# Transposing two raw row tiles on TensorE, with the mean subtracted in PSUM, and first load groups of four feature tiles

## The chip, the cores and the metric

The kernel runs on one core of one Trainium2 chip. The core has five engines with a queue of their own each: TensorE (PE, matmuls; its weight loads are shown as PEld), VectorE (DVE), ScalarE (ACT), GpSimd (POOL) and SyncE (SP), which here only issues DMAs. The engines run side by side and wait for each other through semaphores; each works through its own instructions in the order in which the program gives them. The metric is the device time of one execution in microseconds; lower is better.

## The reference

The input x has 2048 rows of 512 features, in bf16. Its rows are layer-normalized, and two branches run on the normalized rows:

```python
xn = _layernorm(x, axis=-1)
return x + _A_ref(xn, ...) + _B_ref(xn, B_w_gate, B_w_up, B_w_down)

# A: a diagonal state space model, 512 complex states, scanned over the 2048 rows
h = Lam_bar[None, :] * h + Bu[:, t, :]
y = 2.0 * jnp.einsum("blp,dp->bld", hseq, Cmat).real + x * Dskip[None, None, :]
# B: a gated network with 1376 inner features
g = _silu(x @ w_gate)
u = x @ w_up
return (g * u) @ w_down
```

## The kernel before, in words

The 2048 rows are 16 row tiles of 128, and four chunks of four tiles. The 1376 inner features are ten feature tiles of 128 and a rest of 96. For each chunk TensorE does a B projection (`bproj_chunk`, 32 matmuls, L382), the gate and up products (`gateup_chunk`, L457, and L508 for the rest of the features), and the output (`out_chunk`, L569 and L579). VectorE does the statistics, the scans of the state space model with rotations before and after them, and the products of gate and up. ScalarE evacuates PSUM, applies SiLU and computes sines.

Chunk 0 goes another way, so that TensorE can begin early. Its gate and up products take the transposed rows as the stationary operand (`sw_mm`, L484), in three groups of feature tiles (`fgroups`): 0 to 2, 3 to 6 and 7 to 9, so 384, 512 and 384 columns a matmul, 32 matmuls for each group. The weights of the first two groups are loaded in halves. The rows are only centred before they are transposed; the factor 1/std is applied by ScalarE when it evacuates the products (`sw_out`, L493 for the gate with SiLU, L494 for up), and the product of gate and up is taken for two row tiles at a time (L498). These products go to a staging tile `g0` and are transposed by DMA (`g0_dma`, L501).

The head, the code up to the first group's end, is written out by hand. Row tile 0 is summed by VectorE (L227) and centred in two halves as 512 x - sum (L234), which a factor `rs0` takes back later (L701); row tile 1 gets its mean from ScalarE (L230) and is centred by VectorE (L238), as are tiles 2 and 3 with means from the normal statistics (L193, L194). TensorE transposes a centred tile in four blocks (`cT_pe`, L250) and ScalarE copies the result to SBUF (`cT_copy`, L254). Dummy matmuls (L636) keep TensorE busy from the start. The bank allocations rotate through eight PSUM banks; `held` keeps the banks of the first group until `sw_out` reads them. The small vector of parameters is transposed by TensorE (L276) and cast by VectorE (L277); GpSimd takes powers, for 1/std (L203) and for the time steps `dt_t` (L280); VectorE then makes `dre` (L283) and the arguments of the two small sines (`params_sin`, L335 and L337 on ScalarE). The fully normalized rows of chunk 0 (L211) are transposed by DMA (`xT_dma`, L260) for its B projection.

After the head a planner sets the order of VectorE's work. `queue` appends operations with an estimated cost to `backlog`; `pump(us)` is called after each stretch of TensorE work, adds that stretch's length to an account `owed`, and issues operations as long as `owed` is at least half the cost of the next one; `multiply` issues the waiting gate-up products and takes 0.65 from `owed` for each; `need(tag)` issues all that is left up to a tag. Behind the head the list holds: the sine tables of two quarters (L296, L302 to L305), the statistics of row tiles 4 to 7 (`ln1`), their normalization and transpose, and the rest of the tables. Each step of group 1 and group 2 pumps its own TensorE time; each step of a B projection pumps `BP`.

All early loads but three run in SyncE's queue in program order: tile 0, half a gate group, tile 2, half an up group, tile 3, then the second and third groups, row tiles 4 to 7 and the DMA transposes. ScalarE issues tile 1 and two of the halves.

Of the kernel before, what the change touches and what calls it, by code (L numbers as in the profile page):

```python
# [23 lines left out]
def kernel(  # L24
# [17 lines left out]
    nc = tc.nc  # L42
    _, L, D = A_x.shape
# [20 lines left out]
    const = ctx.enter_context(tc.tile_pool(name="const", bufs=1))  # L64
# [9 lines left out]
    def bank(shape=(128, CW), dtype=F32):  # L74
        return psum.tile(list(shape), dtype, name="ps")
# [6 lines left out]
    wg_v = B_w_gate.rearrange("(k p) f -> p k f", p=128)  # L82
    wu_v = B_w_up.rearrange("(k p) f -> p k f", p=128)


    xall = const.tile([128, NT, D], BF16, name="xall")
    xnT = const.tile([128, NCH, KD, CW], BF16, name="xnT")

    fgroups = [(0, 3), (3, 7), (7, FT - 1)]
    wg_g, wu_g = [], []  # L90
    for gi, (a, b) in enumerate(fgroups):
        cols = min(F, b * 128) - a * 128
# [18 lines left out]
    def load_w1(q, tiles, view, gi):  # L111
        a, b = fgroups[gi]
        q.dma_start(out=tiles[gi][:], in_=view[:, :, a * 128:min(F, b * 128)])


    def load_w1_half(q, tiles, view, gi, k0, k1):
        a, b = fgroups[gi]
        q.dma_start(out=tiles[gi][:, k0:k1, :], in_=view[:, k0:k1, a * 128:min(F, b * 128)])

    HK = KD // 2  # L120
    nc.sync.dma_start(out=xall[:, 0, :], in_=x_v[:, 0, :])
    nc.vector.memset(xall[:, 1, 0:2], 0.0)
    nc.scalar.dma_start(out=xall[:, 1, :], in_=x_v[:, 1, :])
    load_w1_half(nc.sync, wg_g, wg_v, 0, 0, HK)
    nc.scalar.preload_act_table_set("silu_and_others")
    load_w1_half(nc.scalar, wg_g, wg_v, 0, HK, KD)
    nc.sync.dma_start(out=xall[:, 2, :], in_=x_v[:, 2, :])
    load_w1_half(nc.scalar, wu_g, wu_v, 0, 0, HK)
    load_w1_half(nc.sync, wu_g, wu_v, 0, HK, KD)
    nc.sync.dma_start(out=xall[:, 3, :], in_=x_v[:, 3, :])  # L130
    for tiles, view in ((wg_g, wg_v), (wu_g, wu_v)):
        load_w1_half(nc.sync, tiles, view, 1, 0, HK)
        load_w1_half(nc.sync, tiles, view, 1, HK, KD)
    load_w1(nc.sync, wg_g, wg_v, 2)
    load_w1(nc.sync, wu_g, wu_v, 2)
    prm_rows = const.tile([128, 128], BF16, name="prm_rows")
# [35 lines left out]
    ident = const.tile([128, 128], BF16, name="ident")  # L172
    make_identity(nc, ident[:])
    jidx = const.tile([128, CW], F32, name="jidx")


# [15 lines left out]
    def ln_stats(n):  # L192
        nc.vector.bn_stats(out=stats[:, n, 0, :], in_=xall[:, n, :])  # L193
        nc.vector.bn_aggr(out=mv[:, n, :], in_=stats[:, n, 0, :])  # L194
# [6 lines left out]
    def ln_rstd(a, b):  # L201
        nc.vector.tensor_scalar(out=ve[:, a:b], in0=mv[:, a:b, 1], scalar1=EPS, scalar2=None, op0=ALU.add)  # L202
        nc.gpsimd.tensor_tensor(out=rstd[:, a:b], in0=ve[:, a:b], in1=neg_half[:, 0:b - a], op=ALU.pow)  # L203
# [20 lines left out]
    rs0 = const.tile([128, 1], F32, name="rs0")  # L224

    def sum_dve(i):
        nc.vector.tensor_reduce(out=sums[:, 0:1], in_=xall[:, i, :], axis=mybir.AxisListType.X, op=ALU.add)  # L227

    def mean_act(i):
        nc.scalar.activation(out=xnT[:, NCH - 1, 0, :], in_=xall[:, i, :], func=ACT.Copy, scale=1.0 / D,  # L230
                             accum_out=sums[:, 1:2])

    def center_by_sum(i, lo, hi):
        nc.vector.tensor_scalar(out=xc[:, i, lo:hi], in0=xall[:, i, lo:hi], scalar1=float(D),  # L234
                                scalar2=sums[:, 0:1], op0=ALU.mult, op1=ALU.subtract)
# [4 lines left out]
    tA = bank((128, 2, KD, 128), BF16)  # L240
    tB = bank((128, 2, KD, 128), BF16)
    warm = bank()

    def cT_tile(i, k):
        return (((tA, 0) if k < HK else (tB, 0)), (tA, 1), (tB, 1), (tA, 0))[i]

    def cT_pe(i, k0=0, k1=KD):
        t, h = cT_tile(i, k0)
        for k in range(k0, k1):
            nc.tensor.transpose(out=t[:, h, k, :], in_=xc[:, i, k * 128:(k + 1) * 128], identity=ident[:])  # L250

    def cT_copy(i, k0=0, k1=KD):
        t, h = cT_tile(i, k0)
        nc.scalar.copy(out=xcT[:, k0:k1, i * 128:(i + 1) * 128], in_=t[:, h, k0:k1, :])  # L254

    def runs(ap):
        return ap.rearrange("p k (i t) -> p (k i) t", t=128)
# [14 lines left out]
    V = nc.vector  # L272

    def prm_transpose():
        pp = tA[:, 1, 0, :]
        nc.tensor.transpose(out=pp, in_=prm_rows[:], identity=ident[:])  # L276
# [210 lines left out]
    def sw_out(gi, i, psg, psu):  # L487
        a, b = fgroups[gi]
        w = (b - a) * 128
        scale = rs0[:] if i == 0 else rstd[:, i:i + 1]  # L490
        if i % 2 == 0:
            u_pair[0, gi] = up_p.tile([128, 2, CW], BF16, name="u2")
        nc.scalar.activation(out=g0[:, a:b, i, :], in_=by_k(psg[:, 0:w]), func=ACT.Silu, scale=scale)  # L493
        nc.scalar.activation(out=u_pair[0, gi][:, i % 2, 0:w], in_=psu[:, 0:w], func=ACT.Copy, scale=scale)  # L494
        if i % 2 == 1:
            g = g0[:, a:b, i - 1:i + 1, :]
            u = u_pair[0, gi][:, :, 0:w].rearrange("p i (f d) -> p f i d", d=128)
            products.append(lambda: V.tensor_tensor(out=g, in0=g, in1=u, op=ALU.mult))  # L498
# [132 lines left out]
    BP = 4 * 0.2163  # L631
    one = nc.const_aps.tensor(1.0, (128, 1), BF16)

    def dummy(n, cols):
        for _ in range(n):
            nc.tensor.matmul(warm[:, 0:cols], lhsT=one.to_broadcast([128, 128]), rhs=one.to_broadcast([128, cols]),  # L636
                             start=True, stop=True)

    def ln_rest(c, on_act):
# [15 lines left out]


    G, U = wg_g, wu_g
    held = [[None, None] for _ in range(TPC)]

    def head_mm(which, i, k0=0, k1=KD):  # L660
        if k0 == 0:
            held[i][which] = bank()
        sw_mm(held[i][which], (G, U)[which], 0, i, k0, k1)

    dummy(7, CW)
    dummy(3, 128)
    sum_dve(0)
    mean_act(1)
    center_by_sum(0, 0, HW)
    center_by_sum(0, HW, D)  # L670
    cT_pe(0, 0, HK)
    cT_copy(0, 0, HK)
    cT_pe(0, HK, KD)
    cT_copy(0, HK, KD)
    center(1, sums[:, 1:2])
    dummy(2, 128)
    cT_pe(1)
    cT_copy(1)
    head_mm(0, 0)
    ln_stats(1)  # L680
    ln_rstd(1, 2)
    ln_stats(2)
    center(2, mv[:, 2, 0:1])
    ln_rstd(2, 3)
    head_mm(0, 1)
# [15 lines left out]
    V.tensor_scalar(out=rs0[:], in0=rstd[:, 0:1], scalar1=1.0 / D, scalar2=None, op0=ALU.mult)  # L701
# [157 lines left out]
```

## Time and profile before

| what | value |
|---|---|
| median of 3 runs (lowest to highest) | 179.48 us (179.46 to 179.9) |
| the profiled execution's own time | 179.06 us |
| its span | 177.1 us |
| TensorE busy | 172.7 us (97%) |
| VectorE busy | 157.4 us (89%) |
| ScalarE busy | 108.5 us (61%) |
| GpSimd busy | 27.8 us (16%) |
| mean DMA rate over the span | 98 GB/s |
| first gate matmul of chunk 0 starts | 5.14 us |
| B projection of chunk 0, of chunk 1 starts | 23.31 us, 31.12 us |

Times within the trace count from the first instruction of the span. The span is shorter than the time of the execution, which also holds what lies around the program. A row of the timeline gives the start, the length, the engine, the line of the code, the operation, what it writes and reads, and how many instructions of the kind follow each other; in square brackets stands the idle time before it with what ended that. A line with a q behind the engine (SPq) is the issue of a DMA, not the transfer.

### The profile page before, as it was taken

To read this page: it belongs to the slowest core of one execution; us is meant where nothing else is said; L and a number is where in the kernel's file an instruction comes from. 1 tells how busy PE (TensorE), PEld (TensorE's weight loads), DVE (VectorE), ACT (ScalarE), POOL (GpSimd) and SP (SyncE) were. 2 spreads that over 40 slices of the span, in tenths; PEclk is the share of its full clock that TensorE was granted. 3 is DMA by queue.
4 is the path that set the end of the run, shared out by engine and by line. 5 is a ranking of instruction groups with operands and counts; after the bars stand their busy time and mean duration, and the time that the engine had idled before them with its cause. 6 is when DMAs were issued, how large, how long until landed. Compare 5 with 4: busy or idle time off the path is not lost.

```text
span 177.1 us, 2357 instructions
## 1 busy us (share of the span) xinstructions
PE 172.7 (97%) x851; PEld 81.9 (46%) x867; DVE 157.4 (89%) x258; ACT 108.5 (61%) x186; POOL 27.8 (16%) x36
## 2 busy tenths in 40 slices
PE   8999999999999999999999999999999999999993
PEld 3554544444444444444444444443444444444743
DVE  3978999999999999999999999999999996899033
ACT  4469998799976697036996660024866659771000
POOL 6370030050000000047000000025000002506100
PEclk9999999999999999999999999999999999999999
DMA  5999998999994000027033000007200002993612
GB/s 167 355 329 215 147 241 164 210 251 231 161 302 178 0 0 4 0 31 84 6 61 62 0 0 0 0 3 88 31 0 2 0 0 16 180 161 37 83 46 76
DMA packets 35115, 17.36 MB, mean 98 GB/s; under 512 B 24960, under 2 KB 35040, under 8 KB 35072
## 3 DMA queue, kind: packets, MB, share of 16 engines
q1 hardware_dynamic: 30672, 13.31, 33.9%
q0 software_dynamic: 3456, 3.28, 14.6%
q10 hardware_dynamic: 976, 0.62, 1.2%
q8 instruction: 7, 0.11, 0.3%
q14 instruction: 4, 0.03, 0.1%
HBM read 8.03 MB, written 5.24 MB: 75 GB/s over the span
## 4 chain that ended last, share of the span: by engine, by line
PE 97%; issue 1%; ACT 0%; DVE 0%
PE ps L457 29%; PE ps L569 22%; PE ps L382 16%; PE ps L579 16%; PE ps L484 10%; PE ps L636 2%; PE ps L508 2%; PE ps L518 1%; PE ps L250 1%; ACT CF L254 0%; DVE xall L582 0%; PE ps L276 0%
## 5 line engine op out<-in xcount | busy, mean ns | idle before, releaser
L569 PE MATMUL ps<-wd_sb,guT 128*128 128x512 bf16 (+4 forms) x195 | 38.6, 355 | 0.2
L457 PE MATMUL ps<-xnT,wg 128*128 128x512 bf16 x120 | 30.8, 380 | 0.1
L457 PE MATMUL ps<-xnT,wu 128*128 128x512 bf16 x114 | 30.0, 379 | 0.2
L424 DVE TENSOR_TENSOR_SCAN g<-r_t,car,u 128x512 bf16<-128x512 f32 x24 | 28.9, 1267 | 0.0
L382 PE MATMUL ps<-xnT,BT 128*128 128x512 bf16 x126 | 28.2, 380 | 0.2
L579 PE MATMUL ps<-CF,wt 128*128 128x512 bf16 (+2 forms) x140 | 28.1, 355 | 0.2
L569 PEld LDWEIGHTS <-guT 128*128 128x128 bf16 (+1 forms) x198 | 18.5, 98 | 19.9
L586 POOL DMA_DIRECT2D out_dram<-res x12 | 10.5, 1043 | 82.6 <-ACT res L585 76.3
L585 ACT CAST res<-ps 128x512 bf16<-128x512 f32 x12 | 7.0, 585 | 25.6 <-PE ps L579 23.3
L471 ACT ACTIVATE guT<-ps 128x512 bf16<-128x512 f32 x30 | 18.0, 601 | 5.1 <-PE ps L457 4.9
L472 ACT CAST u<-ps 128x512 bf16<-128x512 f32 x30 | 17.7, 590 | 5.2 <-PE ps L457 4.8
L384 ACT CAST u<-ps 128x512 bf16<-128x512 f32 x32 | 17.9, 595 | 4.6 <-PE ps L382 4.5
L579 PEld LDWEIGHTS <-wt 128*128 128x128 bf16 x144 | 13.5, 98 | 14.3
L382 PEld LDWEIGHTS <-BT 128*128 128x128 bf16 x128 | 12.5, 98 | 15.1 <-DMA xnT<-xn 0.4
L457 PEld LDWEIGHTS <-wg 128*128 128x128 bf16 x120 | 11.6, 98 | 14.5 <-issue 0.8
L457 PEld LDWEIGHTS <-wu 128*128 128x128 bf16 x120 | 11.7, 98 | 14.2
L541 ACT ACTIVATE xr<-xall,nb,rstd 128x512 bf16<-128x512 bf16 x16 | 11.9, 806 | 4.0 <-DVE xall L549 2.0
L484 PEld LDWEIGHTS <-CF 128*128 128x128 bf16 x96 | 9.1, 98 | 7.7 <-ACT CF L254 0.4
L203 POOL TENSOR_TENSOR rstd<-ve,neg_half 128x1 f32<-128x1 f32 (+1 forms) x7 | 7.8, 1118 | 26.0 <-DVE ve L202 26.0
L484 PE MATMUL ps<-wg,CF 128*128 128x384 bf16 (+1 forms) x47 | 10.7, 344 | 0.1
L484 PE MATMUL ps<-wu,CF 128*128 128x384 bf16 (+1 forms) x48 | 10.6, 344 | 0.0
L582 DVE TENSOR_TENSOR xall<-ps,xall 128x512 bf16<-128x512 f32 (+2 forms) x6 | 3.1, 514 | 8.1 <-remote 5.6
(110 smaller groups left out, 206.7 us busy)
## 6 DMA issues: line engine op xcount, KB each, us to landing
out_dram<-in_A_x_dram SPq DMA_DIRECT2D x1, 1536.0 KB, 7.7
out_dram<-res POOLq DMA_DIRECT2D x12, 128.0 KB, 3.2
out_dram<-xall POOLq DMA_DIRECT2D x3, 512.0 KB, 6.9
wd_sb<-in_B_w_down_dram SPq DMA_DIRECT2D x1, 1280.0 KB, 7.4
xall<-in_A_x_dram SPq DMA_DIRECT2D x1, 1024.0 KB, 6.6
wg<-in_B_w_gate_dram SPq DMA_DIRECT2D x2, 256.0 KB, 4.8
wu<-in_B_w_up_dram SPq DMA_DIRECT2D x2, 256.0 KB, 4.7
xall<-in_A_x_dram SPq DMA_DIRECT2D x1, 512.0 KB, 6.5
```

The lines of the kernel that those rows point to most:

```text
L203: nc.gpsimd.tensor_tensor(out=rstd[:, a:b], in0=ve[:, a:b], in1=neg_half[:, 0:b - a], op=ALU.pow)
L382: nc.tensor.matmul(ps[:], lhsT=BT[:, part, k, q * 128:(q + 1) * 128], rhs=xnT[:, c, k, :], start=(k == 0), stop=(k == KD - 1))
L384: nc.scalar.copy(out=u_tiles[c][:, part, q, :], in_=ps[:])
L424: V.tensor_tensor_scan(out=g()[:, part, q, :], data0=r_t[:, q:q + 1].to_broadcast([128, CW]), data1=u_tiles[c][:, part, q, :], initial=ini ...
L457: nc.tensor.matmul(ps[:fs, lo:hi], lhsT=wslice(groups, fi, k), rhs=xnT[:, c, k, lo:hi], start=(k == 0), stop=(k == KD - 1))
L471: nc.scalar.activation(out=guT[:fs, fi, :], in_=psg[:fs], func=ACT.Silu)
L472: nc.scalar.copy(out=u_pair[c][:fs, fi % 2, :], in_=psu[:fs])
L484: nc.tensor.matmul(ps[:, 0:(b - a) * 128], lhsT=xcT[:, k, i * 128:(i + 1) * 128], rhs=groups[gi][:, k, :], start=(k == 0), stop=(k == KD - 1))
L541: nc.scalar.activation(out=box["xr"][:], in_=xall[:, n, :], func=ACT.Identity, scale=rstd[:, n:n + 1], bias=nb[:, n:n + 1])
L569: nc.tensor.matmul(o[:], lhsT=gu_tiles[c][:fsz[fi], fi, i * 128:(i + 1) * 128], rhs=wd_sb[:fsz[fi], fi, lo:hi], start=(fi == 0), stop=False)
L579: nc.tensor.matmul(o[:], lhsT=w_tiles[c][:, part, q, i * 128:(i + 1) * 128], rhs=CF[:, part, q, lo:hi], start=False, stop=(part == 1 and q ...
L586: nc.gpsimd.dma_start(out=out_v[:, n, lo:hi], in_=res[:, lo:hi], accum_op=ALU.add)
```

## The change

Row tiles 0 and 1 are no longer centred before they are transposed. TensorE multiplies the raw tile by the identity (`cT_mm`, an ordinary matmul into an f32 bank, in place of a transpose into a bf16 one). Then one more matmul (`cT_mean`) subtracts the mean in the same bank: its stationary operand is a constant matrix of -1/512, its moving operand a diagonal matrix that holds the sum of each row, repeated over the blocks. VectorE sums tile 0 and makes its diagonal, ScalarE does both for tile 1. The copies out of PSUM are shared by VectorE and ScalarE. Tile 0 is now scaled like the others, so `rs0` and its instruction go. Tile 2 takes its mean from ScalarE, and its statistics come later. Tiles 2 and 3 are centred by VectorE as before and transposed by ordinary matmuls.

The feature groups become 0 to 3, 4 to 7 and 8 to 9, so 512, 512 and 256 columns a matmul. Both gate halves and both up halves of the first group are loaded by SyncE; ScalarE loads row tile 1 alone. The identity is made first on GpSimd. There are four long dummy matmuls in place of seven. The `sw_out` of tiles 0 to 3 for the first group stand at other places, and with them their products.

```diff
-    fgroups = [(0, 3), (3, 7), (7, FT - 1)]
+    fgroups = [(0, 4), (4, 8), (8, FT - 1)]
...
+    ident = const.tile([128, 128], BF16, name="ident")
+    make_identity(nc, ident[:])
+    minus_mean = const.tile([128, 128], BF16, name="minus_mean")
     nc.sync.dma_start(out=xall[:, 0, :], in_=x_v[:, 0, :])
     nc.vector.memset(xall[:, 1, 0:2], 0.0)
+    nc.vector.memset(minus_mean[:], -1.0 / D)
     nc.scalar.dma_start(out=xall[:, 1, :], in_=x_v[:, 1, :])
+    nc.scalar.preload_act_table_set("silu_and_others")
     load_w1_half(nc.sync, wg_g, wg_v, 0, 0, HK)
-    nc.scalar.preload_act_table_set("silu_and_others")
-    load_w1_half(nc.scalar, wg_g, wg_v, 0, HK, KD)
+    load_w1_half(nc.sync, wg_g, wg_v, 0, HK, KD)
     nc.sync.dma_start(out=xall[:, 2, :], in_=x_v[:, 2, :])
-    load_w1_half(nc.scalar, wu_g, wu_v, 0, 0, HK)
+    load_w1_half(nc.sync, wu_g, wu_v, 0, 0, HK)
     load_w1_half(nc.sync, wu_g, wu_v, 0, HK, KD)
...
+    def sum_act(i):
+        nc.scalar.activation(out=xnT[:, NCH - 1, 0, :], in_=xall[:, i, :], func=ACT.Copy, accum_out=sums[:, i:i + 1])
...
+    def diag_dve(i):
+        nc.vector.tensor_scalar(out=diag[:, i, :], in0=ident[:], scalar1=sums[:, i:i + 1], scalar2=None, op0=ALU.mult)
+
+    def diag_act(i):
+        nc.scalar.activation(out=diag[:, i, :], in_=ident[:], func=ACT.Copy, scale=sums[:, i:i + 1])
...
+    p2, p0, p1 = bank((128, KD, 128)), bank((128, KD, 128)), bank((128, KD, 128))
+    held = [[None, None] for _ in range(TPC)]
+    held[0][0], held[1][0], held[0][1], held[1][1], held[2][0] = (bank() for _ in range(5))
+
+    def cT_mm(ps, src, k, first, stop):
+        nc.tensor.matmul(ps[:, k, :], lhsT=src[:, k * 128:(k + 1) * 128], rhs=ident[:], start=first, stop=stop)
+
+    def cT_mean(ps, i, k0, k1):
+        nc.tensor.matmul(ps[:, k0:k1, :], lhsT=minus_mean[:],
+                         rhs=diag[:, i:i + 1, :].to_broadcast([128, k1 - k0, 128]), start=False, stop=True)
+
+    def cT_copy(copy, ps, i, k0=0, k1=KD):
+        copy(out=xcT[:, k0:k1, i * 128:(i + 1) * 128], in_=ps[:, k0:k1, :])
...
-    dummy(7, CW)
-    dummy(3, 128)
+    warm = held[2][0]
+    dummy(warm, 4, CW)
+    dummy(warm, 3, 128)
     sum_dve(0)
-    mean_act(1)
-    center_by_sum(0, 0, HW)
-    center_by_sum(0, HW, D)
-    cT_pe(0, 0, HK)
-    cT_copy(0, 0, HK)
-    cT_pe(0, HK, KD)
-    cT_copy(0, HK, KD)
-    center(1, sums[:, 1:2])
-    dummy(2, 128)
-    cT_pe(1)
-    cT_copy(1)
+    sum_act(1)
+    diag_dve(0)
+    for k in range(KD):
+        cT_mm(p0 if k < HK else p1, xall[:, 0, :], k, k % HK == 0, False)
+    for k in range(KD):
+        cT_mm(p2, xall[:, 1, :], k, k == 0, False)
+    dummy(warm, 1, 128)
+    cT_mean(p0, 0, 0, HK)
+    cT_copy(V.tensor_copy, p0, 0, 0, HK)
+    cT_mean(p1, 0, HK, KD)
+    diag_act(1)
+    cT_copy(nc.scalar.copy, p1, 0, HK, KD)
+    dummy(warm, 1, 128)
+    cT_mean(p2, 1, 0, KD)
+    cT_copy(V.tensor_copy, p2, 1, 0, HK)
+    cT_copy(nc.scalar.copy, p2, 1, HK, KD)
     head_mm(0, 0)
     ln_stats(1)
+    mean_act(2)
     ln_rstd(1, 2)
-    ln_stats(2)
-    center(2, mv[:, 2, 0:1])
-    ln_rstd(2, 3)
     head_mm(0, 1)
     ln_stats_half(0, 0)
-    head_mm(1, 0, 0, HK)
-    cT_pe(2)
-    cT_copy(2)
-    head_mm(1, 0, HK, KD)
+    center(2, mean2[:])
+    head_mm(1, 0)
+    for k in range(KD):
+        cT_mm(p1, xc[:, 2, :], k, k == 0, k == KD - 1)
+    cT_copy(nc.scalar.copy, p1, 2)
+    head_mm(1, 1)
     ln_stats(3)
     center(3, mv[:, 3, 0:1])
     ln_rstd(3, 4)
-    head_mm(1, 1)
-    prm_transpose()
     ln_stats_half(0, 1)
     ln_rstd(0, 1)
+    ln_stats(2)
+    ln_rstd(2, 3)
+    head_mm(0, 2, 0, HK)
+    for k in range(KD):
+        cT_mm(p0, xc[:, 3, :], k, k == 0, k == KD - 1)
+    cT_copy(nc.scalar.copy, p0, 3)
+    head_mm(0, 2, HK, KD)
+    prm_transpose()
     exp_pool(dt_t[:], ldt)
...
-    V.tensor_scalar(out=rs0[:], in0=rstd[:, 0:1], scalar1=1.0 / D, scalar2=None, op0=ALU.mult)
-    head_mm(0, 2, 0, HK)
-    cT_pe(3)
-    cT_copy(3)
-    head_mm(0, 2, HK, KD)
+    sw_out(0, 0, *held[0])
     head_mm(1, 2)
...
-    for i in range(2):
-        head_mm(0, 3, i * HK, (i + 1) * HK)
-    sw_out(0, 0, *held[0])
+    head_mm(0, 3)
+    sw_out(0, 1, *held[1])
     head_mm(1, 3)
-    sw_out(0, 1, *held[1])
...
-            if gi == 1 and i < 2:
-                sw_out(0, 2 + i, *held[2 + i])
+            if gi == 1 and i == 0:
+                sw_out(0, 2, *held[2])
+                sw_out(0, 3, *held[3])
```

More of the change, by code (lines that the diff above doesn't have):

```diff
@@ L171 @@
     nc.vector.memset(e_t[:], float(np.e))
-    ident = const.tile([128, 128], BF16, name="ident")
-    make_identity(nc, ident[:])
     jidx = const.tile([128, CW], F32, name="jidx")
@@ L223 @@
     sums = const.tile([128, 2], F32, name="sums")
-    rs0 = const.tile([128, 1], F32, name="rs0")
+    diag = const.tile([128, 2, 128], BF16, name="diag")
     def sum_dve(i):
-        nc.vector.tensor_reduce(out=sums[:, 0:1], in_=xall[:, i, :], axis=mybir.AxisListType.X, op=ALU.add)
+        nc.vector.tensor_reduce(out=sums[:, i:i + 1], in_=xall[:, i, :], axis=mybir.AxisListType.X, op=ALU.add)
+    def sum_act(i):
+        nc.scalar.activation(out=xnT[:, NCH - 1, 0, :], in_=xall[:, i, :], func=ACT.Copy, accum_out=sums[:, i:i + 1])
@@ L229, in mean_act @@
     def mean_act(i):
         nc.scalar.activation(out=xnT[:, NCH - 1, 0, :], in_=xall[:, i, :], func=ACT.Copy, scale=1.0 / D,
[L231 to L235, printed above, removed]
+                             accum_out=mean2[:])
+    def diag_dve(i):
+        nc.vector.tensor_scalar(out=diag[:, i, :], in0=ident[:], scalar1=sums[:, i:i + 1], scalar2=None, op0=ALU.mult)
@@ L237, in center @@
+    def diag_act(i):
+        nc.scalar.activation(out=diag[:, i, :], in_=ident[:], func=ACT.Copy, scale=sums[:, i:i + 1])
     def center(i, mean):
         nc.vector.tensor_scalar(out=xc[:, i, :], in0=xall[:, i, :], scalar1=mean, scalar2=None, op0=ALU.subtract)
[L240 to L250, printed above, removed]
@@ L252, in cT_copy @@
-    def cT_copy(i, k0=0, k1=KD):
-        t, h = cT_tile(i, k0)
-        nc.scalar.copy(out=xcT[:, k0:k1, i * 128:(i + 1) * 128], in_=t[:, h, k0:k1, :])
+    mean2 = const.tile([128, 1], F32, name="mean2")
+    p2, p0, p1 = bank((128, KD, 128)), bank((128, KD, 128)), bank((128, KD, 128))
[3 more added lines that the diff above has]
+        nc.tensor.matmul(ps[:, k, :], lhsT=src[:, k * 128:(k + 1) * 128], rhs=ident[:], start=first, stop=stop)
@@ L274, in prm_transpose @@
     def prm_transpose():
-        pp = tA[:, 1, 0, :]
-        nc.tensor.transpose(out=pp, in_=prm_rows[:], identity=ident[:])
+        pp = p1[:, 0, :]
+        nc.tensor.matmul(pp, lhsT=prm_rows[:], rhs=ident[:], start=True, stop=True)
         V.tensor_copy(out=prm[:].rearrange("p t q -> p (t q)"), in_=pp[:, 0:3 * NQ])
@@ L489, in sw_out @@
         w = (b - a) * 128
-        scale = rs0[:] if i == 0 else rstd[:, i:i + 1]
+        scale = rstd[:, i:i + 1]
         if i % 2 == 0:
@@ L632, with dummy @@
     one = nc.const_aps.tensor(1.0, (128, 1), BF16)
-    def dummy(n, cols):
+    def dummy(ps, n, cols):
         for _ in range(n):
-            nc.tensor.matmul(warm[:, 0:cols], lhsT=one.to_broadcast([128, 128]), rhs=one.to_broadcast([128, cols]),
+            nc.tensor.matmul(ps[:, 0:cols], lhsT=one.to_broadcast([128, 128]), rhs=one.to_broadcast([128, cols]),
                              start=True, stop=True)
@@ L657 @@
     G, U = wg_g, wu_g
-    held = [[None, None] for _ in range(TPC)]
     def head_mm(which, i, k0=0, k1=KD):
-        if k0 == 0:
+        if held[i][which] is None:
             held[i][which] = bank()
         sw_mm(held[i][which], (G, U)[which], 0, i, k0, k1)
-    dummy(7, CW)
-    dummy(3, 128)
+    warm = held[2][0]
+    dummy(warm, 4, CW)
+    dummy(warm, 3, 128)
     sum_dve(0)
-    mean_act(1)
-    center_by_sum(0, 0, HW)
-    center_by_sum(0, HW, D)
-    cT_pe(0, 0, HK)
-    cT_copy(0, 0, HK)
-    cT_pe(0, HK, KD)
-    cT_copy(0, HK, KD)
-    center(1, sums[:, 1:2])
-    dummy(2, 128)
-    cT_pe(1)
-    cT_copy(1)
+    sum_act(1)
[14 more added lines that the diff above has]
+    cT_copy(nc.scalar.copy, p2, 1, HK, KD)
     head_mm(0, 0)
     ln_stats(1)
+    mean_act(2)
     ln_rstd(1, 2)
-    ln_stats(2)
-    center(2, mv[:, 2, 0:1])
-    ln_rstd(2, 3)
     head_mm(0, 1)
     ln_stats_half(0, 0)
-    head_mm(1, 0, 0, HK)
-    cT_pe(2)
-    cT_copy(2)
-    head_mm(1, 0, HK, KD)
+    center(2, mean2[:])
[4 more added lines that the diff above has]
+    head_mm(1, 1)
     ln_stats(3)
```

## The prediction

> **What bounds the kernel now.** I read the page first (busy shares and the chain that ended last), then the waits, then the timeline of each engine from 2.8 to 31.6 us, the stretch before and just behind the changed code.
>
> ```profile
> PE 172.7 (97%) x851; PEld 81.9 (46%) x867; DVE 157.4 (89%) x258; ACT 108.5 (61%) x186; POOL 27.8 (16%) x36
> ...
> DVE  3978999999999999999999999999999996899033
> ...
> PE 97%; issue 1%; ACT 0%; DVE 0%
> ```
>
> TensorE (PE) is the bound: 172.7 of 177.1 us, and the chain hardly leaves it. So only two things can move the time: when PE begins its stream in the head, and a wait that opens in it later. But the DVE row shows VectorE nearly as full from slice 3 on: it follows PE as a second, almost saturated chain, and PE needs something from it at one early place. The timeline there:
>
> ```profile
> 25.29 1.38 DVE L211 TENSOR_SCALAR xn<-xall,mv,rstd 128x512 bf16<-128x512 bf16 x4
> 26.58 0.55 DVE L498 TENSOR_TENSOR guT<-guT,u 128x768 bf16<-128x768 bf16 x1
> ...
> 26.69 1.78 SPq L260 DMA_TRANSPOSE xnT<-xn  x1
> ...
> 30.22 1.02 PE L508 MATMUL ps<-xnT,w_last 128*128 128x512 bf16 x4
> ...
> 31.12 0.55 PEld L382 LDWEIGHTS <-BT 128*128 128x128 bf16 x4 [0.36 <-DMA xnT<-xn]
> ```
>
> VectorE ends the normalizing of row tiles 4 to 7 at 26.67; SyncE issues their transpose at 26.69; it lands 4.38 us later (31.07; the other two of its kind take 4.3); PE, whose fourth L508 matmul starts at 30.87 and leaves the array at 31.085, starts the B projection of chunk 1 at 31.12. PE lost 0.04 us, so this meeting has no slack: PE coming earlier gains nothing, VectorE coming later is paid in full. What VectorE does on the way:
>
> ```profile
> 7.06 0.68 DVE L193 BATCH_NORM_STATS2 stats<-xall 128x6 f32<-128x512 bf16 x1
> ...
> 10.09 0.15 DVE L701 TENSOR_SCALAR rs<-rstd 128x1 f32<-128x1 f32 x1 [0.66 <-POOL rstd L203]
> 10.16 1.66 DVE L211 TENSOR_SCALAR CF<-xall,mv,rstd 128x512 bf16<-128x512 bf16 x4
> 11.74 0.14 DVE L283 TENSOR_TENSOR dre<-dt_t,prm 128x4 f32<-128x4 f32 x1
> ...
> 13.06 0.55 DVE L498 TENSOR_TENSOR guT<-guT,u 128x768 bf16<-128x768 bf16 x1
> 13.53 0.88 DVE L296 TENSOR_SCALAR pm<-jidx,ws 128x512 f32<-128x512 f32 x2
> ...
> 16.39 0.56 DVE L498 TENSOR_TENSOR guT<-guT,u 128x768 bf16<-128x768 bf16 x1
> 17.54 0.69 DVE L498 TENSOR_TENSOR guT<-guT,u 128x1024 bf16<-128x1024 bf16 x1 [0.60 <-ACT u L494]
> ...
> 24.75 0.55 DVE L498 TENSOR_TENSOR guT<-guT,u 128x768 bf16<-128x768 bf16 x1
> ```
>
> From 4.25 on it idles only 0.66 and 0.60 us. And ScalarE (ACT), which feeds its products:
>
> ```profile
> 13.11 0.21 ACT L337 ACTIVATE cos<-fc 128x8 f32<-128x8 f32 x1 [0.28 <-DVE fc L321]
> 13.22 0.56 ACT L493 ACTIVATE guT<-ps,rstd 128x384 bf16<-128x384 f32 x1
> ...
> 16.78 0.73 ACT L494 ACTIVATE u<-ps,rstd 128x512 bf16<-128x512 f32 x1
> ```
>
> **PE in the head.** Before, the first gate matmul starts at 5.14 and the B projection of chunk 0 at 23.31.
> Loads first. The windows of 1 us move 286, 269, 331, 347, 340, 375 KB from 2.00 to 8.00, on top of 53 KB before: the DMA engines are full (share 0.97 to 1.09), so bytes decide and not the queue. Tile 3 ends at 1311 KB of the order before (four tiles of 131, four halves of 197), passed at 6.07; it landed at 6.84 (issue 2.64 + 4.2), 0.8 later. With halves of 262 KB it ends at 1573 KB, passed at 6.85: landing about 7.65. The same sum gives 5.3 for the second gate half, 5.7 for tile 2, 6.5 and 7.25 for the up halves. The two halves that move from ACT to SP cost SP two issues of 0.43 us; the loads behind them wait for earlier landings anyway (the issues before stand at 4.53, 5.44 and 6.52, each just behind a landing), so the B transpose stays at about 8 (8.03) and the transpose of tiles 0 to 3 at about 13.7 (13.86, landing 19.95; needed at 22.9, 3 us of cover). Moving the identity first on GpSimd delays the three parameter loads by 0.6 (0.22 + 0.29 and a gap); the last landed at 6.7, wanted at 10.
> Compute: four dummies at 0.427 spacing and three at 0.107 end at 2.8; tile 0 lands at 2.85, tile 1 at 3.14; eight raw transposing matmuls at the 0.107 of the old transposes run to 3.8. Sum of tile 0 ends 3.56 (row 2.87 + 0.69), its diagonal about 0.25 later (256 columns took 0.28), so the mean matmul of 256 columns starts at 3.93 and is out at 4.35. No row copies 256 f32 columns on VectorE: at most 0.42 (the 256-wide addition from PSUM), at least 0.28; I take 0.42. ACT: sum of tile 1 to 3.88, diagonal 0.3 (8 columns took 0.21, 256 took 0.37), copy of p1 done 4.99, then half of p2; p2's mean leaves at 5.1, both copies end at 5.5. The gate matmuls start at 4.9 instead of 5.14, wait 0.1 for the second gate half and 0.1 for the second up half. The head's 32 matmuls are 512 wide now, 6.92 at 0.216 each (12.07 to 12.93 holds four), where 384 at 0.1625 made 5.20. With eight transposes of tiles 2 and 3 and the parameter one (0.056 each) the head ends at 12.55; then 6.92 for group 1 and, in place of 5.20, 32 matmuls of 256 columns for 3.46: chunk 0's projection at 22.9, **0.4 us earlier**. The 256-column cost is 0.108 by halving; weight loads cannot floor it, since transposes with a load each run at 0.055. PSUM banks are free in time by the ACT starts below.
>
> **VectorE to the normalizing of tiles 4 to 7**, the term that decides.
> 1. Statistics of tile 3 start at 7.06 before. After: the copy of p2 ends 5.55, statistics 1, half of 0 and the centring of 2 follow by 7.1 (1.02 + 0.35 + 0.35), and then tile 3 is awaited until 7.65: **+0.6** (+0.05 if it came at 7.1, +0.95 at 8.0).
> 2. From there to `dre`: 4.67 before, with 0.66 of idling for rstd. After, statistics of tile 2 (1.09) fill that idling, `rs0` goes, and GpSimd runs the power for tile 2 and then `dt_t` (0.56 + 1.02) behind them: 4.84, **+0.17**. So `dre` at 12.5.
> 3. Products: tiles 0/1 of group 0 are 1024 wide, to the next start 0.61 (17.54 to 18.15) against 0.47: **+0.14**.
> 4. Tiles 2/3 of group 0: their four ACT steps are issued ahead of group 1's and all stand behind the cosine. By the rows ACT starts them at `dre` + 1.49, three spacings of 0.57 and 0.70: VectorE gets the product at `dre` + 3.93, 16.4, having been ready at `dre` + 2.8. It waits 1.1 instead of the 0.60 before the product at 17.54. Queued behind it are the sine tables, all statistics of 4 to 7 and their normalizing. To the first of these statistics: 18.15 - 11.74 = 6.41 before, and 3.93 + 0.61 + 1.94 (14.45 to 16.39) + 0.61 = 7.09 after. With item 3 in it: **+0.68**.
> 5. The planner. By its rule (step when the time owed reaches half the cost) and its costs, the head pumps nothing, so moving work from group 2 to the head takes 4 x 0.43 us of pumping from ahead of chunk 0's projection. I followed both lists: before, products 0/1 of group 2, nb, four normalizings, product 2/3 (the rows from 24.75 to 26.58). After, the four normalizings come two each in the second and third steps of the projection, so product 2/3 runs first. Both are 512 wide, about 0.34 each from the 768 and 1024 wide ones: 0.68 against 0.47, **+0.21**. ACT has them out by 23.8, VectorE asks at 23.7 and 26.5.
> Sum: 0.6 + 0.17 + 0.68 + 0.21 = **+1.65**: normalizing ends at 28.3, the transpose lands at 32.7, and PE, there at 30.7, waits 2 us. Chunk 1's projection starts at 32.8 instead of 31.12. Nothing behind gives it back: from there every PE row has next to no idling before it, and VectorE's lag to PE stays, with one product fewer to do.
>
> The page's run took 179.06 us (span 177.1); 179.06 + 1.65 = 180.7. It lies 0.42 under the median of 179.48, so against that median I say **181.1 us**, its own range 180.5 to 181.6 by item 1's two ends and 0.2 for the copies.
>
> **A rule against it.** Warm-up by the rows: dummies at 0.427 until 3.7, transposes 0.107 apart from 4.04, 0.055 apart from 4.92: full rate 4.1 us after PE's first matmul at 0.78. The new order gives PE about as unbroken a stretch, only with small matmuls in the place of three dummies, so I keep 4.9. If it were missed, one more such stretch at half rate, from 4.9 to 9, costs PE 2 us: the parameter matmul moves from 10 to 12, VectorE waits for it in front of its normalizing, `dre` comes at 13.45, and the time is 0.95 later, 182.1. The Trainium skill ("TensorE: Matmul & The Clock Gate", Part 1) says that the gate watches a free-running window of about 3.4 us, so that the point of warming depends on its phase; this trace shows one phase only. By that rule alone the loss is possible in either kernel.
>
> **Rivals.**
> A. VectorE is not late: the normalizing of 4 to 7 ends by 26.3, and PE's 0.4 us stands: 179.1. It decides when items 1, 4 and 5 together vanish. For it: PE's head is really shorter. Against: three separate terms, of which the planner's is pure counting. 12%.
> B. The product of tiles 2/3 finds its data (ACT ahead of the cosine), 1.1 us less: 180.0. Against: ACT runs in order and cosine needs `dt_t`. 10%.
> C. Cold clock, 8%, as above; or the one queue delivers tile 3 after 8.3, item 1 at +1.3: 181.8, 4%.
> Forecast: 66%.
>
> The range to 179.7 and 182.2 leaves out A and a little of C. A tenth of a per cent here is 0.18 us; 0.3% (0.54 us) is about what this kernel's measurement can tell from no change. Forecast, B and C are slower, mostly: 85%. A's 179.1 lies within the bound, only its tail is faster: same 9%, faster 6%.
>
> **What would show it.** Right: the chunk 1 wait on xnT at about 2 us; a DVE wait near 15.3 to 16.4 on ACT L494's line; normalizing of 4 to 7 after the last 512-wide product and ending at 28.3; tile 3's statistics waiting for its load; chunk 0's projection at 22.9. Wrong: chunk 1's projection at or before 31.1, or PE idling elsewhere, above all in the head for weights or in group 2 for banks.

## The result, and the profile after

The changed kernel takes 181.44 us (median of 6 runs, 181.07 to 182.15), the kernel before 179.49 us (6 runs, 179.46 to 179.9). The ratio is 1.0107, with a 95% interval of 1.0085 to 1.0129: slower by about 1.1%. The forecast was 181.1 us.

The page of the changed kernel shows first where the chain that ended last now runs, and the group of the B projections with the idle time before it.

```profile
PE 80%; DVE 9%; DMA 5%; SPq 1%; ACT 1%; issue 1%; POOL 1%
...
L388 PE MATMUL ps<-xnT,BT 128*128 128x512 bf16 x126 | 28.2, 379 | 2.0 <-DMA xnT<-xn 1.8
```

Before, 97% of that chain was TensorE. Now a seventh of the span lies on VectorE and on transfers (9% and 5%), and the B projections have 2.0 us of idling before them where they had 0.2. The chain in order of time (start, length, what) says which work stands in front of TensorE. Its pieces between 3.67 and 33 us:

```profile
3.67 4.29 DMA xall<-in_A_x_dram
7.98 0.70 DVE stats L195
...
11.89 0.85 POOL dt_t L286
...
14.32 0.67 ACT guT L499
...
16.75 0.69 DVE guT L504
...
26.84 0.34 DVE guT L504
27.25 1.29 DVE xn L213 x4
28.57 4.42 DMA xnT<-xn
33.03 3.41 PE ps L388 x15
```

Read from the top: the load of row tile 3, its statistics on VectorE, the power for the time steps, ScalarE's evacuations, the product of tiles 2 and 3, then VectorE's list down to the normalizing of tiles 4 to 7, their transpose, and only then TensorE. No matmul of the head is in it. The meeting point in TensorE's own timeline:

```profile
30.19 1.03 PE L514 MATMUL ps<-xnT,w_last 128*128 128x512 bf16 x4
33.03 1.25 PE L388 MATMUL ps<-xnT,BT 128*128 128x512 bf16 x5 [1.81 <-DMA xnT<-xn]
```

TensorE arrives as before and waits 1.81 us; the projection of chunk 1 starts at 33.03 instead of 31.12, which is 1.91 us later, and the span is 1.9 us longer (179.0 against 177.1).

That this one place carries the whole difference shows in all fourteen profiles, of before, after and the twelve kernels below: the span minus the start of chunk 1's projection is 145.96 to 145.98 us in each (before 177.09 - 31.12 = 145.97, after 179.01 - 33.03 = 145.98). Whatever these kernels do ahead of it, the rest takes the same time.

VectorE's timeline after, at the points that the prediction used:

```profile
7.98 0.69 DVE L195 BATCH_NORM_STATS2 stats<-xall 128x6 f32<-128x512 bf16 x1 [0.71 <-DMA xall<-in_A_x_dram]
...
12.76 0.16 DVE L289 TENSOR_TENSOR dre<-dt_t,prm 128x4 f32<-128x4 f32 x1
...
16.75 0.69 DVE L504 TENSOR_TENSOR guT<-guT,u 128x1024 bf16<-128x1024 bf16 x1 [1.12 <-ACT u L500]
...
19.83 0.69 DVE L195 BATCH_NORM_STATS2 stats<-xall 128x6 f32<-128x512 bf16 x1
...
26.75 0.42 DVE L504 TENSOR_TENSOR guT<-guT,u 128x512 bf16<-128x512 bf16 x1
...
27.16 1.38 DVE L213 TENSOR_SCALAR xn<-xall,mv,rstd 128x512 bf16<-128x512 bf16 x4
```

Tile 3's statistics wait 0.71 us for their load; the product of tiles 2 and 3 waits 1.12 us for ScalarE; the last 512-wide product stands ahead of the normalizing. And the head of TensorE:

```profile
4.64 0.59 PE L490 MATMUL ps<-wg,CF 128*128 128x512 bf16 x2
5.67 1.46 PE L490 MATMUL ps<-wg,CF 128*128 128x512 bf16 x6 [0.44 <-ACT CF L260]
6.96 1.27 PE L490 MATMUL ps<-wu,CF 128*128 128x512 bf16 x4
```

It starts half a microsecond earlier (4.64 against 5.14) and stops after two matmuls. The bracket names ScalarE's copy, but that had ended at 4.63; the second gate half landed at 5.63 (issue 1.65 and 4.0 us to landing), and that is what it waited for.

### The profile page after: what moved, and what is told of

Read it like the earlier page. It is cut to its first block, busy times and chain, and to the rows that moved or that the text cites. A ratio compares the mean times of both kernels' runs of the same rounds, so it can differ in the third digit from the quotient of the medians.

```text
span 179.0 us, 2363 instructions
## 1 busy us (share of the span) xinstructions
PE 172.2 (96%) x851; PEld 81.7 (46%) x867; DVE 157.9 (88%) x258; ACT 109.4 (61%) x188; POOL 26.9 (15%) x36
## 4 chain that ended last, share of the span: by engine, by line
PE 80%; DVE 9%; DMA 5%; SPq 1%; ACT 1%; issue 1%; POOL 1%
PE ps L463 29%; PE ps L575 21%; PE ps L585 15%; PE ps L388 12%; DMA xnT<-xn 2%; DMA xall<-in_A_x_dram 2%; DVE stats L195 2%; PE ps L514 1%; DVE guT L504 1%; DVE pm L311 1%; PE ps L524 1%; SPq L118 1%; DVE pm L310 1%; DVE xn L213 1%; ACT guT L499 1%
## 5 line engine op out<-in xcount | busy, mean ns | idle before, releaser
L205 POOL TENSOR_TENSOR rstd<-ve,neg_half 128x1 f32<-128x1 f32 (+1 forms) x7 | 7.3, 1039 | 27.7 <-DVE ve L204 27.7
L490 PE MATMUL ps<-wg,CF 128*128 128x512 bf16 (+1 forms) x48 | 10.8, 343 | 0.4 <-ACT CF L260 0.4
L490 PE MATMUL ps<-wu,CF 128*128 128x512 bf16 (+1 forms) x47 | 10.7, 343 | 0.1
L195 DVE BATCH_NORM_STATS2 stats<-xall 128x6 f32<-128x512 bf16 x15 | 10.1, 672 | 0.7 <-DMA xall<-in_A_x_dram 0.7
```

The lines of the kernel that those rows point to most:

```text
L490: nc.tensor.matmul(ps[:, 0:(b - a) * 128], lhsT=xcT[:, k, i * 128:(i + 1) * 128], rhs=groups[gi][:, k, :], start=(k == 0), stop=(k == KD - 1))
```

## The experiments

All are compared with the kernel before, run on the same chip beside them (its median there was 179.53 to 179.69); "chunk 1" is the start of its B projection in the profile, "normalized" the end of the normalizing of tiles 4 to 7. The changed kernel was not run again beside them, so an experiment is set against it by their ratios to the kernel before; its 181.44 is the highest of the kernels with the wide groups, the others that keep the planner's list lie at 180.56 to 181.07.

| kernel | median us | ratio, 95% interval | tile 3 landed | normalized | chunk 1 |
|---|---|---|---|---|---|
| before | 179.49 | | 6.88 | 26.67 | 31.12 |
| after | 181.44 | 1.0107 (1.0085 to 1.0129) | 7.96 | 28.54 | 33.03 |
| e1 TensorE 0.86 later | 180.87 | 1.0076 (1.0055 to 1.0097) | 7.80 | 28.38 | 32.90 |
| e2 tile 3 loaded earlier | 181.06 | 1.0080 (1.0058 to 1.0102) | 6.42 | 28.83 | 33.35 |
| e3 normalizing first | 179.51 | 0.9999 (0.9984 to 1.0015) | 8.56 | 23.97 | 31.66 |
| e4 the same in before | 179.61 | 1.0001 (0.9985 to 1.0017) | 7.63 | 21.36 | 31.54 |
| e5 groups and queue alone | 181.07 | 1.0093 (1.0070 to 1.0115) | 8.43 | 28.85 | 33.37 |
| e6 transposes and orders alone | 179.38 | 0.9994 (0.9983 to 1.0006) | 6.76 | 26.58 | 31.03 |
| e7 evacuations spaced | 181.06 | 1.0092 (1.0060 to 1.0125) | 8.45 | 28.88 | 33.38 |
| e8 last product behind | 180.56 | 1.0068 (1.0046 to 1.0090) | 7.81 | 28.06 | 32.56 |
| e9 e6 and e3 together | 179.51 | 0.9999 (0.9982 to 1.0015) | 7.31 | 22.28 | 31.30 |
| e10 two queues, groups of four | 181.06 | 1.0088 (1.0067 to 1.0109) | 8.05 | 28.64 | 33.12 |
| e11 e2, parameters earlier | 180.82 | 1.0073 (1.0054 to 1.0092) | 6.66 | 28.50 | 33.00 |
| e12 e9, late load behind | 179.26 | 0.9984 (0.9971 to 0.9997) | 6.84 | 22.02 | 31.18 |

**e1: is TensorE's head on the path?** The last matmuls of the head are done twice; the result stays the same.

```diff
     head_mm(1, 3)
+    head_mm(1, 3)
     params_sin()
```

> The kernel after, with the last four up matmuls of the head (tile 3, group 0) done twice: 0.86 us more of TensorE work in the head, same result. Theory 1 (the lost time is the wait of chunk 1's projection for VectorE's normalizing of tiles 4 to 7, TensorE arrives 1.8 us too early): no change to the kernel after, 181.4 within 0.3, chunk 1's projection again near 33.0, the wait before it down from 1.81 to about 0.95. Rival (the head's length on TensorE, loads and weights, sets the end): 0.86 later, 182.3.

180.87 us: 0.57 below the changed kernel, more than the 0.3 that I allowed, with intervals that overlap, and not slower. TensorE's timeline in e1:

```profile
30.91 1.03 PE L514 MATMUL ps<-xnT,w_last 128*128 128x512 bf16 x4
32.90 0.60 PE L388 MATMUL ps<-xnT,BT 128*128 128x512 bf16 x2 [0.97 <-DMA xnT<-xn]
```

The last matmuls ahead of the wait came 0.72 later, the wait shrank from 1.81 to 0.97, and the projection began no later (32.90 against 33.03). The rival's 182.3 is excluded.

**e2: tile 3 ahead of the up halves.**

```diff
+    nc.sync.dma_start(out=xall[:, 3, :], in_=x_v[:, 3, :])
     load_w1_half(nc.sync, wu_g, wu_v, 0, 0, HK)
     load_w1_half(nc.sync, wu_g, wu_v, 0, HK, KD)
-    nc.sync.dma_start(out=xall[:, 3, :], in_=x_v[:, 3, :])
```

> The kernel after, with row tile 3 loaded ahead of the two up halves. Theory 1: tile 3 lands near 6.9 instead of 7.96, its statistics start as soon as VectorE is free (7.26 instead of 7.98), everything to the normalizing of tiles 4 to 7 moves with it: 0.7 earlier, 180.7, although the up weights land 0.4 later. Rival (weights bound the head): 0.3 to 0.4 later than after, 181.8.

Tile 3 landed at 6.42 and its statistics began 0.75 earlier, as meant. But the normalizing of 4 to 7 ended at 28.83, no earlier than in the changed kernel: my expectation fell. VectorE's timeline of e2 shows why:

```profile
7.23 0.69 DVE L195 BATCH_NORM_STATS2 stats<-xall 128x6 f32<-128x512 bf16 x1
...
11.59 0.17 DVE L283 COPY prm<-ps 128x12 f32<-128x12 f32 x1 [1.23 <-PE ps L282]
...
13.12 0.17 DVE L289 TENSOR_TENSOR dre<-dt_t,prm 128x4 f32<-128x4 f32 x1
```

VectorE waited 1.23 us for the parameter matmul, which stands on TensorE behind the up products, and their weights now landed later (8.62 instead of 7.60 for the second half). The 0.7 did not vanish, it changed its place. TensorE's head is thus not quite off VectorE's path: in the changed kernel the parameter matmul is out at 10.46 and copied at 11.04, so it has 0.6 us of slack there, not the 1.8 of the meeting point.

**e11: e2, with the parameter matmul out of that place**, and into another bank.

```diff
-        pp = p1[:, 0, :]
+        pp = p0[:, 0, :]
...
     center(2, mean2[:])
+    prm_transpose()
     head_mm(1, 0)
...
     head_mm(0, 2, HK, KD)
-    prm_transpose()
```

> As e2 (tile 3 loaded ahead of the up halves), and the parameter matmul moved ahead of the first up matmuls, so that VectorE does not wait for it behind them. Theory 4 (in e2 the gain went into the wait for the parameter matmul, 1.23): that wait goes; the next to hold the normalizing is the transposing of tile 3 on TensorE near 11.0 and the power on GpSimd, dre near 12.35 instead of 13.12 in e2, normalizing of tiles 4 to 7 ends near 28.1: 0.7 less than e2, 180.4 to 180.7. Rival (late up weights hold VectorE in another way): as e2, 181.06.

The 1.23 us are gone, and `dre` came at 12.72, against 13.12 in e2 and an expected 12.35. VectorE's timeline of e11:

```profile
7.75 0.17 DVE L283 COPY prm<-ps 128x12 f32<-128x12 f32 x1 [0.29 <-PE ps L282]
7.83 0.68 DVE L195 BATCH_NORM_STATS2 stats<-xall 128x6 f32<-128x512 bf16 x1
...
12.72 0.17 DVE L289 TENSOR_TENSOR dre<-dt_t,prm 128x4 f32<-128x4 f32 x1 [0.25 <-POOL dt_t L286]
```

Half of the expected gain: the copy waits 0.29 ahead of the statistics, which stand at 7.83, and GpSimd's power has become the next wait. The median, 180.82, lies 0.24 under that of e2 with intervals that overlap, so the direction rests on the profile alone. Against the changed kernel e11 gains next to nothing: tile 3 lands 1.30 earlier (6.66), but `dre` comes at 12.72 against 12.76, and the normalizing ends at 28.50 against 28.54. Tile 3's statistics begin only 0.15 earlier than there (7.83 against 7.98), behind the copy that waits for TensorE. So no kernel with the wide groups gets back by an earlier tile 3 what its late landing seems to cost in the timeline.

**e3 and e4: the normalizing of tiles 4 to 7 ahead of all tables**, in the changed kernel and in the one before.

```diff
-    queue("tables", tables[:2])
-    queue("ln1", stats1)
-    queue("tables", tables[2:4])
-    queue("ln1", norm1)
-    queue("tables", tables[4:])
+    queue("ln1", stats1 + norm1)
+    queue("tables", tables)
```

> The kernel after, with the planner's list reordered: statistics and normalizing of tiles 4 to 7 ahead of all sine tables (5.4 us of VectorE work move behind the normalizing). Theory 1: the wait before chunk 1's projection goes, TensorE runs through as it arrives (31.15): 1.8 to 1.9 less, 179.5 to 179.7. Rival (VectorE as a whole is the second bound, so that the tables pushed back open a wait of their own before chunk 0's state space part, or bank waits): 180.3 to 181.4, with a new idle stretch on TensorE after 31.

> The kernel before, with the same reordering of the planner's list. Theory 1: only 0.04 us of waiting stood there, so no change, 179.4 to 179.6. Rival (the normalizing was already binding before, or the table order is worth something by itself): more than 0.5 us away from 179.5.

The pair answers the main question. In the changed kernel the reordering takes away all of the loss: 179.51, no longer to be told from the kernel before. In the kernel before it is worth nothing, 179.61. So what the change costs is VectorE's lateness at this place, and before the change VectorE was just not late. No wait came up later (the rest is 145.98 and 145.97). But the transpose did not land as early as it was issued; SyncE's and the weight load's rows in e3:

```profile
24.00 4.80 SPq L266 DMA_TRANSPOSE xnT<-xn  x1
```

```profile
31.51 0.47 PEld L388 LDWEIGHTS <-BT 128*128 128x128 bf16 x3 [0.18 <-DMA xnT<-xn]
```

Issued at 24.00, landed at 31.46: 7.5 us, where the changed kernel took 4.4. In e4 it was 22.59 to 31.02. This is taken up by e12.

**e5 and e6: one part of the change at a time.** e5 is the kernel before with the new groups and all halves in SyncE's queue; e6 is the changed kernel with the old groups and the old spread of loads.

```diff
-    fgroups = [(0, 3), (3, 7), (7, FT - 1)]
+    fgroups = [(0, 4), (4, 8), (8, FT - 1)]
...
-    load_w1_half(nc.scalar, wg_g, wg_v, 0, HK, KD)
+    load_w1_half(nc.sync, wg_g, wg_v, 0, HK, KD)
...
-    load_w1_half(nc.scalar, wu_g, wu_v, 0, 0, HK)
+    load_w1_half(nc.sync, wu_g, wu_v, 0, 0, HK)
```

> The kernel before with the groups of four and the loads in SyncE's queue, its own transposes and orders kept. Theory 2 (most of the loss comes with the loads and groups: tile 3 lands near 7.7, ScalarE's and VectorE's steps on group 0 get wider, one product of group 2 goes ahead of the normalizing): normalizing of tiles 4 to 7 ends near 27.9 (0.6 for the landing, 0.4 for ScalarE's wider steps, 0.2 for the product), chunk 1's projection at 32.3, 180.6 to 180.9. Rival (the transposes and the new order of the head cost it): 179.5 to 179.8.

> The kernel after with the old groups (384, 512, 384 columns) and the old spread of loads over two queues; raw transposes and the new orders kept. Theory 2: tile 3 lands near 7, normalizing of tiles 4 to 7 ends near 27.0 to 27.3 (0.2 for the later dre, the four early evacuations keep a wait), 179.7 to 180.1. Rival (the transposes and the order cost it): 180.6 to 181.4.

The loss goes with the groups: e5 has 181.07, all of it within the intervals, and e6 has 179.38, no loss. (e5 came out above its 180.6 to 180.9 and e6 below its 179.7; in the profiled executions tile 3 landed late in e5, at 8.43, and early in e6, at 6.76, which fits.) Neither run parts the three groups from each other: their sizes change together. VectorE's timeline of e5:

```profile
13.29 0.14 DVE L283 TENSOR_TENSOR dre<-dt_t,prm 128x4 f32<-128x4 f32 x1
...
18.37 0.69 DVE L498 TENSOR_TENSOR guT<-guT,u 128x1024 bf16<-128x1024 bf16 x1 [0.29 <-ACT u L494]
...
20.14 0.69 DVE L193 BATCH_NORM_STATS2 stats<-xall 128x6 f32<-128x512 bf16 x1
```

From `dre` to the first statistics of tiles 4 to 7 it needs 6.85 us, where the kernel before needed 6.41 with the same order. VectorE's timeline of e6:

```profile
11.56 0.16 DVE L289 TENSOR_TENSOR dre<-dt_t,prm 128x4 f32<-128x4 f32 x1
...
15.13 0.56 DVE L504 TENSOR_TENSOR guT<-guT,u 128x768 bf16<-128x768 bf16 x1 [0.83 <-ACT u L500]
```

The product of tiles 2 and 3 waits here too, 0.83 us, but for evacuations of 384 columns, and from `dre` to the end of the normalizing e6 needs 15.02 us, like the kernel before (14.93) and unlike the changed one (15.78). Chunk 0's projection began at 23.00 in e6, against 23.31 before; but with the same head it began at 23.53 in e9 and at 23.41 in e12, so a gain of TensorE by the raw transposes is not shown.

**e7: the evacuations of tiles 2 and 3 at their old places.**

```diff
-            if gi == 1 and i == 0:
-                sw_out(0, 2, *held[2])
-                sw_out(0, 3, *held[3])
+            if gi == 1 and i < 2:
+                sw_out(0, 2 + i, *held[2 + i])
```

> The kernel after with the evacuations of tiles 2 and 3 of group 0 spaced as before (one in each of the first two steps of group 1). The long wait of VectorE at 16.75 (1.12) goes and shorter ones come behind the first table: ScalarE has the second product of group 1 out at dre + 6.2 at best. Theory: 0.3 less, normalizing ends near 28.2, 181.1. Rival (the wait is worth its full length): 1.0 to 1.1 less, 180.4.

VectorE's timeline of e7:

```profile
13.25 0.16 DVE L289 TENSOR_TENSOR dre<-dt_t,prm 128x4 f32<-128x4 f32 x1
...
18.40 0.69 DVE L504 TENSOR_TENSOR guT<-guT,u 128x1024 bf16<-128x1024 bf16 x1 [0.29 <-ACT u L500]
19.56 0.69 DVE L504 TENSOR_TENSOR guT<-guT,u 128x1024 bf16<-128x1024 bf16 x1 [0.47 <-ACT u L500]
20.17 0.69 DVE L195 BATCH_NORM_STATS2 stats<-xall 128x6 f32<-128x512 bf16 x1
```

The wait of 1.12 goes and two of 0.29 and 0.47 come: from `dre` to the first of these statistics 6.92 us instead of 7.07. The wait is worth 0.15, a seventh of its length, probably since ScalarE has to make the same eight wider evacuations in either order. The time, 181.06, says nothing on so small a term, as tile 3 landed at 8.45 in the profiled execution.

**e8: the last product of group 2 kept back by one step of the planner.**

```diff
             pump(2 * KD * cols / CW * 0.2163)
-            multiply(0)
+            multiply(1 if (gi, i) == (2, TPC - 1) else 0)
```

> The kernel after with the last product of group 2 kept back by one step, so that it comes behind the planner's next step. Theory: the account is 0.65 higher at that point, so nb and two of the normalizings are issued ahead of it or just beside it; at most the product's 0.34 moves behind the normalizing: 0.1 to 0.35 less, normalizing ends 28.2 to 28.45, 181.1 to 181.3. Rival (the planner's order is without weight): 181.4.

VectorE's timeline of e8:

```profile
26.68 1.38 DVE L213 TENSOR_SCALAR xn<-xall,mv,rstd 128x512 bf16<-128x512 bf16 x4
27.97 0.42 DVE L504 TENSOR_TENSOR guT<-guT,u 128x512 bf16<-128x512 bf16 x1
```

The product now comes behind the normalizing; `dre` to its end takes 15.44 instead of 15.78, 0.34 less, the upper end of what was expected. The time, 180.56, is lower than that by more than the product is worth, but its interval overlaps the one of the changed kernel.

**e10: two queues with the groups of four.**

```diff
-    load_w1_half(nc.sync, wg_g, wg_v, 0, HK, KD)
+    load_w1_half(nc.scalar, wg_g, wg_v, 0, HK, KD)
...
-    load_w1_half(nc.sync, wu_g, wu_v, 0, 0, HK)
+    load_w1_half(nc.scalar, wu_g, wu_v, 0, 0, HK)
```

> The kernel after with groups of four kept, and second gate half and first up half loaded from ScalarE's queue again, as in the kernel before. Theory 3 (bytes ahead of tile 3 decide, not the queue): tile 3 still lands between 7.5 and 8.2, no change, 181.1 to 181.5. Rival (the one queue is what makes tile 3 late): it lands near 7.0, dre near 11.9, 180.4 to 180.6.

VectorE's timeline of e10:

```profile
8.08 0.69 DVE L195 BATCH_NORM_STATS2 stats<-xall 128x6 f32<-128x512 bf16 x1 [0.59 <-DMA xall<-in_A_x_dram]
```

Tile 3 landed at 8.05 and the time is 181.06: the queue is not the cause, the wider halves ahead of tile 3 are. Over the profiled executions tile 3 landed at 7.80 to 8.56 behind the wide groups (seven kernels that load it last) and at 6.76 to 7.63 behind the narrow ones (five). The Trainium skill ("Trainium Kernel Development and Optimization", Key Constraints) says that queues of several engines run on the same 16 DMA engines, and that issuing from more than one saves only issue time; e10 agrees in that two queues did not bring tile 3 earlier.

**e9 and e12: a version that beats both?** e9 joins e6 and e3. e12 moves one load behind the transpose of tiles 4 to 7 in addition.

```diff
     load_last()
-    load_late()
...
     need("ln1")
+    load_late()
     g0_dma(0, fgroups[1][1])
```

> Raw transposes with the old groups and two load queues (as in e6), and the planner's list with statistics and normalizing of tiles 4 to 7 ahead of the tables (as in e3). Theory 1: e6 had TensorE ready for chunk 1 at 30.8 and xnT landing at 30.99, so TensorE's gain of the head (chunk 0's projection at 23.0 instead of 23.3) is let through: 179.1 to 179.3, 0.2 to 0.3 below the kernel before. Rival (a later wait on VectorE takes it back): 179.4 to 179.6.

> As e9 (raw transposes, old groups and queues, normalizing first), and the 1 MB load of tiles 8 to 15 issued behind the transpose of tiles 4 to 7 instead of ahead of it. In e3, e4 and e9 the transpose was issued at 22.6 to 24.0 and still landed at 30.9 to 31.5, 2.5 us behind that load. Theory 5 (the load ahead of it in SyncE's queue is a second floor near 31.0): the transpose lands 4.4 us behind its issue, near 27.1, and TensorE never waits there; the time is then the head of TensorE alone, 179.0 to 179.5. Rival (the transpose is slow for another reason): it lands again at 30.9 or later, 179.5.

e9 gave nothing, 179.51. SyncE's timeline in e9, then in e12:

```profile
22.13 0.51 SPq L160 DMA_DIRECT2D xall<-in_A_x_dram  x1
22.74 5.49 SPq L266 DMA_TRANSPOSE xnT<-xn  x1
```

```profile
22.05 1.80 SPq L266 DMA_TRANSPOSE xnT<-xn  x1
23.90 1.14 SPq L160 DMA_DIRECT2D xall<-in_A_x_dram  x1
```

Behind the 1 MB load the issue of the transpose holds the queue for 5.49 us and it lands at 30.89; ahead of the load it is issued in 1.80 us and lands at 26.41. So there was a second floor near 31 us, by transfers, just under VectorE's. But TensorE lost nothing to it in the profiled execution of e9:

```profile
30.43 1.03 PE L514 MATMUL ps<-xnT,w_last 128*128 128x512 bf16 x4
31.30 1.46 PE L388 MATMUL ps<-xnT,BT 128*128 128x512 bf16 x6
```

It went from one to the other without a wait, and chunk 1 began 0.41 after the transpose had landed, since chunk 0's projection had begun only at 23.53. e12 takes 179.26 us, with a ratio to the kernel before of 0.9984 (0.9971 to 0.9997): the only version whose interval lies below 1, by 0.16%. It is one of twelve kernels, its interval overlaps that of e9 (0.9982 to 1.0015), and chunk 0's projection began at 23.41 in its profile. So the runs show that the floor was moved, but not that a shorter time came of it.

## Why the prediction was right, and where not

The direction, the place and the size were right: 181.1 forecast, 181.44 measured, by the mechanism that was named, VectorE's late normalizing of tiles 4 to 7. Its terms, in us of delay against the kernel before, from the two profiled executions:

| step | predicted | measured |
|---|---|---|
| 1. statistics of tile 3 begin | 0.6 (0.05 to 0.95) | 7.98 - 7.06 = 0.92 |
| 2. from there to `dre` | 0.17 | 4.78 - 4.68 = 0.10 |
| 3 and 4. from `dre` to the statistics of 4 to 7 | 0.68 | 7.07 - 6.41 = 0.66 |
| 5. from there to the end of the normalizing | 0.21 | 8.71 - 8.52 = 0.19 |
| sum | 1.65 | 1.87 |
| chunk 1's projection | 32.8 | 33.03 |

- Step 1 was undersized. Tile 3 landed at 7.96, not at 7.65. The rule used (bytes ahead of it at the rates of the kernel before) names a cause that e5, e6 and e10 bear out, but the landing scatters by 0.8 us between executions with the same load order, which one trace could not show. It also is only one of two gates: e2 shows that the parameter matmul behind the up weights takes over when tile 3 comes early, and e11 that opening this gate too gains nothing. Three small slips: the steps added to 5.55 give 7.27, not 7.1 (VectorE was free at 7.27), so the low end of this term should have been 0.2; tile 3 landed at 6.88 before, not 6.84; and the four terms as written add up to 1.66.
- Steps 2 to 5 came within 0.1 each. The planner's part (5), pure counting of costs, was exact in order and nearly in size, and e8 confirms it by taking it away.
- Step 4's wait of 1.1 was measured as 1.12, but by e7 it is not a loss of that size: spaced evacuations bring back 0.15. So the forecast had the size right but leaned on the new order, where most of it is the widening from 384 to 512 columns: with the old order and the wide groups e5 already has 0.44 of the 0.66 (6.85 - 6.41). Steps 3 to 5 together were forecast as 0.89 and measured as 0.85; e6, with the old groups, has 0.09.
- "0.4 us earlier" on TensorE is the step that failed: chunk 0's projection began at 23.29, against 23.31 before. The first gate matmul came even earlier than forecast, 4.64 for 4.9 (4.65 to 5.07 in the other ten kernels with raw transposes, so 4.64 was an early one), but TensorE waited 0.60 for the second gate half instead of 0.1 and 0.24 for the second up half instead of 0.1. In no profile with the wide groups did the projection begin before 23.29. It had no effect on the time, because 1.8 us of waiting stood behind it (e1).
- Rival A (179.1) and B (180.0) are out by the time. The half rate of C was seen in other executions, but for a shorter time than its stretch from 4.9 to 9: in e7 the rate doubled 2.8 us later than in the changed kernel, at 6.62, and `dre` still came 4.78 us behind the statistics of tile 3, as there. C's price of 0.95 us was not put to the test. Its other half, tile 3 behind 8.3, came up too (8.43 to 8.56 in e3, e5 and e7), but with two queues e10 has tile 3 at 8.05 as well, so the one queue is not shown to be behind it.
- "Nothing behind gives it back" holds to 0.02 us, by the 145.96 to 145.98 us that are left in every profile.

Subtracting the mean in PSUM, with the orders that came with it, costs nothing that e6 could tell (0.9983 to 1.0006); what costs is the new group sizes. By the timelines the wider first group makes tile 3 late and the products wider, and the shorter last one puts a product ahead of the normalizing; no run tried one group alone.

## What to carry to other kernels

A chain that is 97% one engine still has meeting points with the second engine, and it is there that a change is paid: look for the wait of 0.04 us that shows two chains arriving together, and add up what the change does to the other one. Wider groups at the front of a load order delay what is loaded behind them, here from one queue and from two alike; ask which later instruction needs the last small load, and what the engines do meanwhile. Where a planner fills gaps by a running account, moving work from a pumped to an unpumped place moves other work past a deadline, and that can be counted by hand.

## What the runs showed of the hardware that I had not expected

- The rate of matmuls doubles at very different times for the same order of instructions in the head. In the changed kernel the mean matmuls of 256 columns are 0.108 apart from 3.83 on. In e7, whose head is the same, the gate matmuls are still 0.426 apart at 5.41 and 0.216 apart only from 6.62 on:

```profile
4.98 2.67 PE L490 MATMUL ps<-wg,CF 128*128 128x512 bf16 x8
```

  Eight in 2.67 us, where the changed kernel has six in 1.46. In e8, e9, e10 and e11, too, the first gate matmuls, near 5.0, ran at half rate. The granted clock of the profile is 1.00 from 3 to 8 us in both e7 and the changed kernel, so here the spacing of the starts tells the rate and the clock row does not. The Trainium skill ("TensorE: Matmul & The Clock Gate", Part 1) puts the doubling down to a free-running window of about 3.4 us and gives 0.5 us either way for the spread of the transition. The 2.8 us between these two executions are more than that spread and less than the window; no run here shows the window itself.
- A DMA transpose issued behind a 1 MB load in the same queue held SyncE for 5.49 us instead of 1.80 and landed 8.15 us after its issue instead of 4.36 (e9 against e12). With the load ahead of it, the earlier issue in e3, e4 and e9 brought the landing to 31.46, 31.02 and 30.89, against 31.07 in the kernel before.
- The end of the head's loads scatters by 0.8 us between executions of the same load order: with narrow groups at 6.76 to 7.63, with wide ones in one queue at 7.80 to 8.56.
